# Three chained layers on one Trainium2 core: how v's scales are spread, and where w_in is decoded

## The chip, the cores and the metric

The program runs on one core of one Trainium2 chip. The metric is the device time of one execution in microseconds, as the median of three runs. The engines are named PE (matrix products), DVE (VectorE), ACT (ScalarE), POOL (GpSimd) and SP (the engine that issues nearly all DMA here, in program order).

## The reference

Three layers follow one another; the output of one is the input of the next. Four batches, 448 positions, 768 columns.

```python
# 1: attention, 12 heads of 64, mixing heads before and after the softmax
scores = scale * (q @ k.transpose(0, 1, 3, 2))
scores = np.einsum('bhij,hg->bgij', scores, w_pre)
attn = softmax(scores)
attn = np.einsum('bhij,hg->bgij', attn, w_post)
x = attn @ v
# 2: moe1
h = gelu_tanh(x @ w_in)
u, v = h[..., :512], h[..., 512:]
v_n = (v - mean(v)) / sqrt(var(v) + 1e-06) * g_ln
v_s = np.einsum('ts,bsd->btd', w_sg, v_n) + b_sg
x = x + (u * v_s) @ w_out
# 3: moe2
theta = x @ w_theta
y = np.einsum('ts,bsd->btd', w_tok_r, x * cos(theta)) + np.einsum('ts,bsd->btd', w_tok_i, x * sin(theta))
u = x + y
out = u + np.maximum(u @ w_ch, 0.0)
```

Five of the weights (w_in, w_out, w_theta, w_tok and w_ch) come as 64-bit floats and are turned on the chip into pairs of 32-bit tiles, a high and a low part, since a product takes three matmuls with them (high by high, high by low, low by high).

## The kernel before

**Attention** (function `attention`) goes through 180 blocks of up to 10 query rows by 12 heads. A block passes a chain of helpers, and the step loop (L437) issues in step s the helpers of several blocks at once, each with its own lookahead: `relayout(s+7)` (L217, a DMA that puts the scores of a block with heads on partitions), `premix(s+4)` (PE, L223, mixes heads) with `rowmax` (DVE nmx, L229), `expo(s+3)` (ACT e, L236), `recip2` and `p_hi(s+2)` (POOL ph, L255), `p_lo(s+1)` (DVE pl, L262), `postmix(s)` (PE, L277 to L280) and `at_hi`, `at_lo(s-1)` (ACT ah L302, DVE al L308). `attn_v` (L329) multiplies by v once a row of blocks is complete; `turn_x` and `store_x` transpose the result and store it to DRAM (xT). The lists `early`, `work` and `late` put other work into steps, and `tail` holds what stands in the steps relative to the last block, NB.

**v** is scaled for each batch and column by a power of two, so that a 16-bit high and low part hold it. `v_max` (L148) takes maxima of a transposed copy vT, with the columns on partitions; `v_scale` makes the scale sv, 128 partitions by 6. Scaling needs it along the free axis of all partitions. So `v_scale_out` (L162) writes sv to DRAM as 768 single elements, and `v_scale_in` (L166) reads them back to all 128 partitions as vbc. Then `v_mul` (POOL, L178), `v_hi` (ACT, L181) and `v_lo` (POOL, L185) make the two parts; in these steps lie what the prediction calls the stretches with v.

**Decode jobs** (class `Dense`, L573 to L631) each turn 128 by 256 numbers: a load (draw, L588), two ACT operations (L599, L600), two on DVE (L602, L604), one on DVE (L610), an ACT copy of the high part with a product on DVE or POOL (L615, L618), two on POOL (L624, L625), and, for jobs without a place of their own in SBUF, a store to DRAM (L631). Fourteen jobs stand beside attention, one each 11.6 steps: the 12 of the second half of w_in, and 2 of the first. They store to win_d in DRAM. The others are issued by `tick`, where each tick advances a pipeline whose steps lie apart by the numbers in LAGS; 15 ticks stand on the last steps of attention (5 before NB and on), and the tables TV, TU, TG and TO say how many follow each unit of moe1.

**moe1** (function `moe1`) is a list of units, which PE takes in order: `v_chunk` and `u_half` (w_in's second and first half), `gate` (w_sg), `out` (w_out), by batch. At the handover SP loads the second half of w_in back (`load_win`, L660), and x from xT (`load_x`, L742 and L744). **moe2** follows with theta, tok and ch; nearly all of it is matmuls.

Of the kernel before, what the change touches and what calls it, by code (L numbers as in the profile page):

```python
# [6 lines left out]
F32 = mybir.dt.float32  # L7
F32R = mybir.dt.float32r
# [9 lines left out]
NP = H // 2  # L18
DM = H * D
# [18 lines left out]
def attention(tc, nc, io, xT, B, extra, tail):  # L38
# [17 lines left out]
    with ExitStack() as es:  # L56
# [45 lines left out]
        ident = cp.tile([TI, TI], F32, name="ident")  # L102

        def consts():
            kpost = sm_p.tile([TI, H, IB], F32, tag="kpost", name="kpost", bufs=1)
            nc.sync.dma_start(out=kpost, in_=io["kpost"].rearrange("p (g i) -> p g i", g=H))
            nc.sync.dma_start(out=ident, in_=io["ident"][:TI, :TI])
# [33 lines left out]
        vs_dram = es.enter_context(tc.tile_pool(name="a_vsd", bufs=1, space=bass.MemoryType.DRAM))  # L141
        vs_d = vs_dram.tile([B, DM], F32, name="vs_d")
# [220 lines left out]
        def put(d, s, fn, *a):  # L363
            d.setdefault(s, []).append((fn, a))
# [119 lines left out]
TV = ((0, 1, 3, 1), (2, 2, 2, 2), (2, 1, 2, 2), (0, 1, 2, 0))  # L484
TU = ((2, 1, 0, 1), (2, 0, 2, 1), (2, 0, 2, 1), (3, 0, 2, 1))
TG = ((1, 0, 1, 0), (2, 1, 0, 1), (0, 1, 0, 1), (0, 1, 0, 0))
TO = ((2, 1, 1, 0, 1, 1), (0, 1, 0, 0, 2, 0), (0, 1, 1, 0, 0, 1), (0, 1, 1, 3, 2, 2))
KE = 1
# [5 lines left out]
LAGS = ((5, 7), (4, 5), (3, 4), (2, 3), (1, 2), (0, 0))  # L494
# [169 lines left out]
def moe1(d, left, right):  # L664
# [6 lines left out]
    def start():  # L671
# [6 lines left out]
        d.raw_bufs, d.mid_bufs, d.out_bufs = 3, 4, 4  # L678
# [8 lines left out]
        for k in range(KE, KD):  # L687
            def tiles(k=k):
                win[k, 0] = pair("win", HF, f"win{k}_0")
                return win[k, 0]  # L690
            d.jobs += d.decode_tiles(io["w_in"], slice(128 * k, 128 * k + 128), 0, HF, tiles)
        d.jobs += [None]
# [9 lines left out]
    def rest():  # L702
        tail_ps.close()
        for name, bufs in (("w", 1), ("u", 1), ("vn", 1), ("t", 2), ("dec", 1)):
            d.open(name, bufs, left)
        d.open_psum(8, right)
        w = d.pools["w"]
        gln = w.tile([128, KF], F32, name="gln")
        with nc.allow_non_contiguous_dma(reason="512 values"):
            nc.sync.dma_start(out=gln, in_=io["g_ln"].rearrange("(k p) -> p k", p=128))  # L710
# [9 lines left out]
    def load_win(k, half):  # L720
        win[k, half] = d.load_pair(d.pools["win"], d.win_d, slice(128 * k, 128 * k + 128),
                                   slice(HF * half, HF * half + HF), f"win{k}_{half}")
# [222 lines left out]
    return tail, win_es, g0[B - 1] - 1, end  # L945


def moe2(d, left, win_es, last_u, m1_left):
# [227 lines left out]
def build(tc, nc, io, out):  # L1176
    with tc.manual_schedule(), ExitStack() as top:
# [5 lines left out]
        right, left1, left2 = ExitStack(), ExitStack(), ExitStack()  # L1183
        tail, win_es, last_u, end = moe1(d, left1, right)
# [3 lines left out]
        jobs = d.decode_all(io["w_in"], HF, DFF, d.win_d)  # L1188
        jobs += d.decode_all(io["w_in"], 0, HF, d.win_d, 128 * KE)
# [4 lines left out]
        right.close()  # L1194
        left2.close()


def layout(i):
# [9 lines left out]
    for x in range(IB):  # L1208
# [14 lines left out]
        "g_ln": f(i["moe_g_ln"]),  # L1223
# [26 lines left out]
```

## Time and profile before

| | |
|---|---|
| median of 3 runs | 1046.14 us (1044.67 to 1046.32) |
| the profiled execution | 1047.47 us, its span 1045.6 us |
| mean granted clock of PE | 0.978 |
| PE busy | 982.3 us (94%) |
| DVE, POOL, ACT busy | 775.5, 622.4, 586.6 us |
| chain that ended last, by engine | PE 57%, DVE 20%, DMA 9%, POOL 5% |

PE is busy almost all of the time. An average over the whole span hides where it isn't, so the views below go by stretch: 0 to 60 us is the start, 60 to 470 the body of attention, 470 to 580 the handover and the first units of moe1, 580 to 740 the rest of it. From 800 on it is moe2.

### The profile page before, as it was taken

How to read it: one execution, taken by the hardware profiler on the slowest of the kernel's cores; microseconds unless marked ns; L12 is line 12 of the kernel's file. 1: busy time of each engine (PE TensorE's matmuls, PEld its weight loads, DVE VectorE, ACT ScalarE, POOL GpSimd, SP SyncE). 2: the span in 40 equal slices, each digit the busy share in tenths (PEclk: the TensorE clock that was granted, in tenths of full speed). 3: DMA queues.
4: the chain of work that ended last, by engine and by line, in shares of the span. 5: the costliest groups of instructions: out<-in, count | busy, mean ns of one | idle time of the engine just before them, and what ended most of it. 6: DMA issues, size and time to landing. Idle time of an engine off the chain costs nothing.

```text
span 1045.6 us, 21830 instructions
## 1 busy us (share of the span) xinstructions
PE 982.3 (94%) x7848; PEld 742.7 (71%) x7848; DVE 775.5 (74%) x1458; ACT 586.6 (56%) x1374; POOL 622.4 (60%) x818
## 2 busy tenths in 40 slices
PE   7789999999999999997978999799999999999998
PEld 2445655565656555566756979587888999999997
DVE  2799878987888878985989998898896724925611
ACT  4577778786777778775754645454364412613310
POOL 0596558754686548854656877775666643753622
PEclk9899999999999999998989999999999999999999
DMA  5757565556556564347353676758956131130021
GB/s 191 154 167 221 142 139 183 180 168 129 161 193 203 131 158 152 131 108 265 113 155 89 213 225 199 229 188 274 335 184 226 41 106 31 32 106 16 31 76 53
DMA packets 135504, 159.47 MB, mean 153 GB/s; under 512 B 30309, under 2 KB 120933, under 8 KB 135397
## 3 DMA queue, kind: packets, MB, share of 16 engines
q1 hardware_dynamic: 135397, 158.08, 50.3%
q8 instruction: 63, 1.03, 0.4%
q14 instruction: 44, 0.36, 0.1%
HBM read 86.66 MB, written 32.85 MB: 114 GB/s over the span
## 4 chain that ended last, share of the span: by engine, by line
PE 57%; DVE 20%; DMA 9%; POOL 5%; issue 4%; ACT 3%; SPq 1%; DVEq 0%; ACTq 0%; POOLq 0%
PE ps L564 27%; PE psB L223 10%; PE psA L203 5%; PE psD L329 5%; DVE da L604 3%; PE psC L280 3%; PE psC L277 3%; DMA blk<-s 2%; PE psC L278 2%; DVE pl L262 2%; DVE da L602 2%; DVE dp L610 2%; DMA xres<-xT 2%; DVE dp L618 2%; DMA xraw<-xT 1%
## 5 line engine op out<-in xcount | busy, mean ns | idle before, releaser
L255 POOL TENSOR_SCALAR ph<-e,rc 120x448 f16<-120x448 f32 x180 | 163.9, 911 | 147.3 <-DVE rc L250 99.8
L223 PE MATMUL psB<-blk,kpre 120*120 120x448 f32 x360 | 177.3, 575 | 13.0 <-DMA blk<-s 8.2
L229 DVE TENSOR_REDUCE nmx<-psB 120x1 f32<-120x448 f32 x180 | 111.3, 618 | 49.9 <-PE psB L223 40.8
L262 DVE SCALAR_TENSOR_TENSOR pl<-e,rc,ph 120x448 f16<-120x448 f32 x180 | 147.4, 819 | 0.0
L236 ACT ACTIVATE e<-psB,nmx 120x448 f32<-120x448 f32 x180 | 114.3, 635 | 43.1 <-DVE nmx L229 43.0
L308 DVE SCALAR_TENSOR_TENSOR al<-psC,ah 128x480 f16<-128x480 f32 x180 | 116.1, 645 | 8.2 <-ACT ah L302 7.9
L277 PE MATMUL psC<-wh,ph 120*128 120x120 f16 x720 | 97.7, 218 | 10.9 <-DVE al L308 7.1
L302 ACT ACTIVATE ah<-psC 128x480 f16<-128x480 f32 x180 | 103.0, 572 | 7.6 <-PE psC L280 4.9
L209 ACT ACTIVATE s<-psA 120x896 f32<-120x896 f32 (+1 forms) x90 | 82.5, 917 | 42.5 <-PE psA L203 41.1
L564 PE MATMUL ps<-wtok,z 128*128 128x448 f32 x504 | 104.8, 368 | 0.4 <-POOL z L560 0.4
L564 PEld LDWEIGHTS ps<-wtok,z 128*128 128x128 f32 x504 | 94.4, 188 | 10.1 <-POOL z L560 0.8
L277 PEld LDWEIGHTS <-ph 120*128 120x128 f16 x720 | 68.8, 99 | 44.3 <-issue 18.6
L278 PE MATMUL psC<-wl,ph 120*128 120x120 f16 x720 | 97.1, 218 | 2.4 <-issue 2.4
L329 PEld LDWEIGHTS <-ah 128*128 128x128 f16 x1536 | 76.6, 99 | 31.2 <-issue 31.2
L203 PE MATMUL psA<-k,q 64*120 64x448 f32 (+1 forms) x384 | 96.2, 580 | 1.0 <-ACT s L209 1.0
L564 PE MATMUL ps<-wth,x2s 128*128 128x384 f32 x504 | 92.5, 338 | 2.0 <-POOL x2s L560 2.0
L564 PE MATMUL ps<-u,wch 128*128 128x448 f32 x432 | 89.9, 368 | 0.0
L564 PEld LDWEIGHTS ps<-wth,x2s 128*128 128x128 f32 x504 | 87.2, 188 | 2.8 <-POOL x2s L560 2.6
L560 POOL TENSOR_TENSOR z<-zz,z 128x384 fp32r<-128x384 f32 x56 | 61.9, 1125 | 45.8 <-ACT z L557 45.8
L564 PEld LDWEIGHTS ps<-u,wch 128*128 128x128 f32 x432 | 81.0, 188 | 8.1
L278 PEld LDWEIGHTS <-ph 120*128 120x128 f16 x720 | 71.2, 99 | 14.4 <-issue 14.2
L329 PE MATMUL psD<-vl,ah 128*128 128x64 f16 x768 | 78.0, 194 | 1.1 <-POOL vl L185 1.1
(124 smaller groups left out, 2171.9 us busy)
## 6 DMA issues: line engine op xcount, KB each, us to landing
blk<-s SPq DMA_DIRECT2D x176, 210.0 KB
draw<-in_w_in SPq DMA_DIRECT2D x24, 256.0 KB
vraw<-in_vN SPq DMA_DIRECT2D x24, 256.0 KB
k<-in_kvT SPq DMA_DIRECT2D x24, 224.0 KB
vT<-in_kvT SPq DMA_DIRECT2D x12, 448.0 KB
xraw<-xT SPq DMA_DIRECT2D x24, 224.0 KB
xres<-xT SPq DMA_DIRECT2D x24, 224.0 KB
x2T<-xres SPq DMA_DIRECT2D x24, 224.0 KB
```

The costliest lines, as they stand in the source:

```text
L203: nc.tensor.matmul(ps[e][:n, :S], q[p, o:o + n], k[p], start=True, stop=True)
L223: nc.tensor.matmul(ps[:r, :S], kpre[:r, :r], sblk.pop(s)[:r], start=True, stop=True)
L229: nc.vector.tensor_reduce(out=m[:r], in_=mix[s][:r, :S], axis=AX.X, op=ALU.max, negate=True)
L236: nc.scalar.activation(out=e[:r], in_=mix.pop(s)[:r, :S], func=AF.Exp, bias=nmx.pop(s)[:r], accum_out=sm[:r])
L255: nc.gpsimd.tensor_scalar(out=p[:r], in0=ex[s][0][:r], scalar1=rec[s][:r], scalar2=0.0, op0=ALU.mult, op1=ALU.add)
L262: nc.vector.scalar_tensor_tensor(out=p[:r], in0=ex.pop(s)[0][:r], scalar=rec.pop(s)[:r], in1=ph[s][:r], op0=ALU.mult, op1=ALU.subtract)
L277: nc.tensor.matmul(ps[:, jc, :, :n], cols(a, jc), wh[:r, :, :n], start=(jc == 0), stop=False)
L278: nc.tensor.matmul(ps[:, jc, :, :n], cols(a, jc), wl[:r, :, :n], start=False, stop=False)
L302: nc.scalar.activation(out=at_view(s, at[b, t][0]), in_=src, func=AF.Copy, scale=2.0 ** -17)
L308: nc.vector.scalar_tensor_tensor(out=al, in0=src, scalar=2.0 ** -17, in1=ah, op0=ALU.mult, op1=ALU.subtract)
L329: nc.tensor.matmul(ps[:, o:o + 64], a[:, i0:i0 + 128], v[:, jc, 64 * e:64 * e + 64], start=(o == 0 and m == 0), stop=(o == 320 and m == le ...
L564: self.nc.tensor.matmul(ps, l, r, start=(i == 0), stop=(i == len(terms) - 1))
```

## The change

v's scales no longer go through DRAM. `v_diag` writes them onto the diagonals of six 128x128 tiles (ACT), and `v_spread` multiplies these by a tile of ones in two matmuls of 384 columns, each followed by an ACT copy from PSUM (buffer psT, one of it) to vbc. vT is loaded two steps later at the start, and its maxima stand in steps -2 to 0.

All 24 jobs of w_in stand beside attention. The 12 of the second half come first and write their tiles straight into SBUF, in a new pool w1 that is open from the beginning; for such jobs the product of L618 is always on DVE. The 12 of the first half still store to win_d, and six loads bring them back, two steps apart, at steps NB-4 to NB+6. Three ticks are left on attention's last steps, w_out's jobs come first there, and the tables are spread anew. The pool w1 later holds the first half of w_theta and the last 128 columns of w_ch. g_ln comes transposed, so that its load is contiguous. Middle buffers of the jobs are 3 for 4, output buffers 5 for 4.

```diff
-        def v_scale_out(b):
-            with nc.allow_non_contiguous_dma(reason="768 scales"):
-                nc.sync.dma_start(out=vs_d[b].rearrange("(c p) -> p c", p=128), in_=raws.pop(("sv", b)))
-
-        def v_scale_in(b):
-            bc = vsc_p.tile([128, DM], F32, tag="vbc", name="vbc", bufs=1)
-            nc.sync.dma_start(out=bc, in_=vs_d[b].partition_broadcast(128))
-            vsb[b] = bc
+        def v_diag(b):
+            sv = raws.pop(("sv", b))
+            raws["dg", b] = vsc_p.tile([128, NP, 128], F32R, tag="dg", name="dg", bufs=1)
+            for c in range(NP):
+                nc.scalar.activation(out=raws["dg", b][:, c], in_=ident, func=AF.Copy, scale=sv[:, c:c + 1])
+
+        def v_spread(b):
+
+            dg = raws.pop(("dg", b))
+            vsb[b] = vsc_p.tile([128, DM], F32, tag="vbc", name="vbc", bufs=1)
+            for half in range(2):
+                ps = psD.tile([128, 512], F32, tag="psT", name="psV", bufs=1)
+                nc.tensor.matmul(ps[:, :384], ones, dg[:, 3 * half:3 * half + 3], start=True, stop=True)
+                nc.scalar.activation(out=vsb[b][:, 384 * half:384 * half + 384], in_=ps[:, :384], func=AF.Copy)
...
             put(late, s, v_scale, b)
-            put(early, s + 2, v_scale_out, b)
-            put(early, s + 5, v_scale_in, b)
+            put(late, s + 1, v_diag, b)
+            put(work, s + 2, v_spread, b)
...
-            put(early, -LD + c // 2, load_vT, 0, c)
-            put(late, -LD + 1 + c // 2, v_max, 0, c)
-        put_v(0, -LD + 4, VM, 2)
+            put(early, -LD + 2 + c // 2, load_vT, 0, c)
+            put(late, -2 + c // 2, v_max, 0, c)
+        put_v(0, 1, VM, 2)
...
-LAGS = ((5, 7), (4, 5), (3, 4), (2, 3), (1, 2), (0, 0))
+LAGS = ((5, 6), (4, 4), (2, 3), (3, 3), (1, 2), (0, 0))
...
-        d.raw_bufs, d.mid_bufs, d.out_bufs = 3, 4, 4
+        d.raw_bufs, d.mid_bufs, d.out_bufs = 3, 3, 5
...
+    def decode_win():
+
+        jobs = []
+        for k in range(KD):
+            def tiles(k=k):
+                t = d.pools["w1"].tile([128, 2, HF], F32R, tag=f"w1_{k}", name=f"win{k}_1")
+                win[k, 1] = t[:, 0], t[:, 1]
+                return win[k, 1]
+            jobs += d.decode_tiles(io["w_in"], slice(128 * k, 128 * k + 128), HF, DFF, tiles)
+        return jobs + d.decode_all(io["w_in"], 0, HF, d.win_d)
...
-        at(-6 + k // 3, load_win, k, 1)
+        at(-4 + 2 * k, load_win, k)
         at(-6 + k // 2, load_x, 0, k)
         at(-5 + k // 2, split_x, 0, k)
-    for k in range(KE):
-        at(-4, load_win, k, 0)
-    for i in range(17 - 2 * KE):
-        at(-6 + KE + i, d.tick)
+    for i in range(3):
+        at(5 + 2 * i, d.tick)
...
-        jobs = d.decode_all(io["w_in"], HF, DFF, d.win_d)
-        jobs += d.decode_all(io["w_in"], 0, HF, d.win_d, 128 * KE)
```

Three places show how the order moves. First SP at the start, from the last load of vT on; vs_d and vbc are the two ends of the round trip, draw the first decode job's load. Before:

```order
L133 DMA vT<-in_kvT 128x2x448
L217 DMA blk<-s 120x1x448 x4
L162 DMA vs_d<-sv 128x6x1
L217 DMA blk<-s 120x1x448 x2
L588 DMA draw<-in_w_in 128x512
L217 DMA blk<-s 120x1x448
L166 DMA vbc<-vs_d 128x768
L217 DMA blk<-s 120x1x448
L173 DMA vraw<-in_vN 128x4x128
```

and after:

```order
L135 DMA vT<-in_kvT 128x2x448
L223 DMA blk<-s 120x1x448 x4
L593 DMA draw<-in_w_in 128x512
L223 DMA blk<-s 120x1x448 x2
L179 DMA vraw<-in_vN 128x4x128
L223 DMA blk<-s 120x1x448
L140 DMA q<-in_qT 128x720
```

The two issues of the round trip are gone from between the blk issues. Next SP at the handover, from the last blk on; win_1 is the second half of w_in, win_0 the first, xraw a piece of x. Before:

```order
L217 DMA blk<-s 96x1x448
L685 DMA ident<-in_ident 128x128
L660 DMA win_1_9143<-win_d 128x2x512
L742 DMA xraw<-xT 128x448
L744 DMA xraw<-xT 128x64
L660 DMA win_1_9148<-win_d 128x2x512
```

and after:

```order
L752 DMA xraw<-xT 128x64
L665 DMA win_0_9464<-win_d 128x2x512
L750 DMA xraw<-xT 128x448
L752 DMA xraw<-xT 128x64
L750 DMA xraw<-xT 128x448
L752 DMA xraw<-xT 128x64
L364 DMA xT<-x 128x3x120
L665 DMA win_0_9550<-win_d 128x2x512
L665 DMA win_0_9620<-win_d 128x2x512
```

The loads of x now go first, and the loads of w_in that are left are those of the first half, further back. Last DVE just before the first wsg (the spatial gate's weight, made there); da and dp are operations of decode jobs, v the normalised half of moe1. Before:

```order
L618 TENSOR_TENSOR dp<-dp,dl 128x256
L610 TENSOR_SCALAR dp<-da 128x256
L782 RECIPROCAL sd<-sd 128x4
L618 TENSOR_TENSOR dp<-dp,dl 128x256
L602 TENSOR_SCALAR da<-dp 128x256
L604 SCALAR_TENSOR_TENSOR da<-dp,da 128x256
L787 TENSOR_SCALAR v<-v,mv,sd 128x512 x2
L610 TENSOR_SCALAR dp<-da 128x256
L602 TENSOR_SCALAR da<-dp 128x256
L604 SCALAR_TENSOR_TENSOR da<-dp,da 128x256
L787 TENSOR_SCALAR v<-v,mv,sd 128x512 x2
L560 TENSOR_TENSOR wsg<-wsgraw,wsg 128x448 x2
```

and after:

```order
L781 BN_STATS bst<-v 128x6
L784 BN_AGGR mv<-bst 128x2
L790 RECIPROCAL sd<-sd 128x4
L795 TENSOR_SCALAR v<-v,mv,sd 128x512 x2
L607 TENSOR_SCALAR da<-dp 128x256
L609 SCALAR_TENSOR_TENSOR da<-dp,da 128x256
L795 TENSOR_SCALAR v<-v,mv,sd 128x512 x2
L565 TENSOR_TENSOR wsg<-wsgraw,wsg 128x448 x2
```

Between the last nmx and this wsg DVE has the first two operations of 12 jobs before and of 1 after; from there to the first xres it is 12 before and 14 after, and from xres to the end 48 and 47.

## Rows read from the trace of the kernel before

**Rows 1.** busy time by stretch: length, engines (instructions), TensorE clock, DMA share, GB/s

```profile
0.00:60.00 60.00, 46.54 (x244) 21.01 (x244) 33.30 (x75) 32.52 (x68) 20.86 (x37) 0.94 0.61 164
60.00:470.00 410.00, 393.65 (x4684) 239.77 (x4682) 346.40 (x717) 314.03 (x755) 265.15 (x430) 1.00 0.56 162
470.00:580.00 110.00, 91.45 (x689) 74.95 (x687) 92.60 (x173) 62.54 (x158) 64.11 (x75) 0.89 0.50 157
580.00:740.00 160.00, 151.20 (x673) 127.44 (x672) 139.32 (x228) 80.64 (x194) 120.42 (x137) 0.97 0.72 230
```

**Rows 2.** timeline of SP near the first scale round trip: start, length, issue

```profile
26.74 0.38 SPq L162 DMA_DIRECT2D vs_d<-sv  x1
...
36.90 0.35 SPq L166 DMA_DIRECT2D vbc<-vs_d  x1
```

**Rows 3.** PE timeline, batches 0 and 1: start, length, [idle before <- releaser]

```profile
38.57 1.82 PE L223 MATMUL psB<-blk,kpre 120*120 120x448 f32 x2 [5.38 <-DMA blk<-s]
...
143.48 0.98 PE L223 MATMUL psB<-blk,kpre 120*120 120x448 f32 x2 [0.95 <-DMA blk<-s]
```

**Rows 4.** busy time by stretch, at the scales of batches 0, 2, 3

```profile
38.00:44.00 6.00, 5.43 (x27) 3.43 (x28) 3.49 (x8) 1.88 (x6) 1.28 (x2) 0.50 1.01 257
254.00:258.00 4.00, 1.85 (x14) 0.80 (x12) 0.00 (x0) 0.56 (x2) 0.80 (x2) 1.00 0.59 107
370.00:374.00 4.00, 2.02 (x23) 1.24 (x21) 0.43 (x3) 1.22 (x5) 0.95 (x2) 1.00 0.51 95
```

**Rows 5.** timeline of DVE at the start, before the first block

```profile
19.80 1.09 DVE L148 TENSOR_REDUCE vmx<-vT 128x2 f32<-128x896 f32 x1 [7.20 <-DMA vT<-in_kvT]
...
22.94 0.61 DVE L229 TENSOR_REDUCE nmx<-psB 120x1 f32<-120x448 f32 x1
```

**Rows 6.** groups of instructions, 60 to 470 us: busy us, mean ns | idle

```profile
L333 ACT ACTIVATE xi<-psD 120x384 f32<-120x384 f32 (+1 forms) x28 | 13.7, 490 | 11.9 <-PE psD L329 11.9
L625 POOL TENSOR_TENSOR dh<-da,dp 128x256 fp32r<-128x256 f32 x13 | 12.5, 964 | 1.0
...
L624 POOL TENSOR_TENSOR da<-da,dh 128x256 f32<-128x256 f32 x13 | 9.4, 726 | 1.0
...
L604 DVE SCALAR_TENSOR_TENSOR da<-dp,da 128x256 uint32<-128x256 uint32 x13 | 7.5, 575 | 0.4
...
L602 DVE TENSOR_SCALAR da<-dp 128x256 uint32<-128x256 uint32 x13 | 5.6, 433 | 0.7 <-ACT dp L599 0.7
...
L618 DVE TENSOR_TENSOR dp<-dp,dl 128x256 f32<-128x256 f32 x5 | 4.2, 845 | 0.0
L610 DVE TENSOR_SCALAR dp<-da 128x256 uint32<-128x256 uint32 x13 | 3.7, 283 | 0.0
```

**Rows 7.** the page, costliest groups: one row

```profile
L564 PE MATMUL ps<-wth,x2s 128*128 128x384 f32 x504 | 92.5, 338 | 2.0 <-POOL x2s L560 2.0
```

**Rows 8.** chain of waits, 186 to 194 us: start, length, what

```profile
187.31 1.29 DVE da L602
...
188.63 0.74 DVE da L604
```

**Rows 9.** timeline of POOL, the same place

```profile
186.79 1.65 POOL L178 TENSOR_TENSOR vraw<-vraw,vbc 128x512 f32<-128x512 f32 x1
```

**Rows 10.** busy time by stretch, one with v work and one without

```profile
160.00:200.00 40.00, 37.36 (x383) 21.42 (x379) 35.17 (x67) 31.10 (x81) 32.80 (x46) 0.96 0.50 158
200.00:250.00 50.00, 50.00 (x632) 31.18 (x629) 43.00 (x94) 39.41 (x91) 26.93 (x50) 1.00 0.65 178
```

**Rows 11.** PE's waits, 470 to 492 us: total, times, longest

```profile
PE psC L277 <- DVE al L308: 7.1, 2, 5.1
```

**Rows 12.** busy time by stretch, handover and first gates

```profile
484.00:492.00 8.00, 6.07 (x54) 5.49 (x53) 2.50 (x5) 2.75 (x5) 3.76 (x5) 0.51 1.06 374
531.00:548.00 17.00, 10.82 (x31) 7.15 (x30) 16.83 (x23) 11.31 (x28) 13.49 (x14) 0.70 0.38 117
```

**Rows 13.** timeline of PE at the first output matmul of moe1

```profile
570.24 7.10 PE L564 MATMUL ps<-g,wout 128*128 128x448 f32 x26 [3.33 <-POOL wout L625]
```

More of the change, by code (lines that the diff above doesn't have):

```diff
@@ L101, in attention @@
         dwp = cp.tile([128, NP], F32, name="dwp")
-        ident = cp.tile([TI, TI], F32, name="ident")
+        ident = cp.tile([128, 128], F32, name="ident")
+        ones = cp.tile([128, 128], F32R, name="ones")
         def consts():
@@ L106, in consts @@
             nc.sync.dma_start(out=kpost, in_=io["kpost"].rearrange("p (g i) -> p g i", g=H))
-            nc.sync.dma_start(out=ident, in_=io["ident"][:TI, :TI])
+            nc.sync.dma_start(out=ident, in_=io["ident"])
+            nc.scalar.activation(out=ones, in_=ident, func=AF.Copy, scale=0.0, bias=1.0)
             wrep = sm_p.tile([128, H, H], F32, tag="wrep", name="wrep", bufs=1)
@@ L140, in attention @@
         vt, dsc, vsb = {}, {}, {}
-        vs_dram = es.enter_context(tc.tile_pool(name="a_vsd", bufs=1, space=bass.MemoryType.DRAM))
-        vs_d = vs_dram.tile([B, DM], F32, name="vs_d")
         def v_max(b, c):
@@ L483 @@
 E_G = ('PPPV', 'VVPP', 'VPVP', 'VVPV')
[L484 to L488, printed above, removed]
+TV = ((), (2, 2, 2), (1, 1, 1, 1), (1, 1, 1))
+TU = ((1, 1, 1, 1), (2, 1, 2, 1), (2, 1, 2, 1), (2, 1, 2, 1))
+TG = ((1, 1, 1, 1), (0, 1, 0, 1), (0, 1, 0, 1), (0, 0, 0, 0))
+TO = ((1, 1, 1, 1, 1, 1), (1, 1, 1, 1, 1, 1), (1, 1, 1, 0, 1, 1), (0, 0, 1, 1, 1, 1))
 MAGIC = 12582912.0
@@ L686, in start @@
         pair = lambda pool, n, tag: [d.pools[pool].tile([128, n], F32R, tag=f"{tag}_{i}", name=tag) for i in range(2)]
[L687 to L692, printed above, removed]
         for k in range(KF):
@@ L708, in rest @@
         gln = w.tile([128, KF], F32, name="gln")
-        with nc.allow_non_contiguous_dma(reason="512 values"):
-            nc.sync.dma_start(out=gln, in_=io["g_ln"].rearrange("(k p) -> p k", p=128))
+        nc.sync.dma_start(out=gln, in_=io["g_ln"])
         bsg = w.tile([128, S], F32, name="bsg")
@@ L718, in rest2, with load_win @@
             d.open(name, bufs, left)
-    def load_win(k, half):
-        win[k, half] = d.load_pair(d.pools["win"], d.win_d, slice(128 * k, 128 * k + 128),
-                                   slice(HF * half, HF * half + HF), f"win{k}_{half}")
+    def load_win(k):
+        win[k, 0] = d.load_pair(d.pools["win"], d.win_d, slice(128 * k, 128 * k + 128), slice(0, HF), f"win{k}_0")
+    def decode_win():
[7 more added lines that the diff above has]
+        return jobs + d.decode_all(io["w_in"], 0, HF, d.win_d)
     def load_wsg(c):
@@ L944, in moe1 @@
         at(8 + c // 2, norm, 0, c)
-    return tail, win_es, g0[B - 1] - 1, end
+    return tail, decode_win(), win_es, g0[B - 1] - 1, end
 def moe2(d, left, win_es, last_u, m1_left):
@@ L958, in load_wth @@
     def load_wth(k, half):
-        wth[k, half] = d.load_pair(d.pools["th"], d.wth_d, slice(128 * k, 128 * k + 128),
-                                   slice(384 * half, 384 * half + 384), f"wth{k}_{half}")
+        rows = slice(128 * k, 128 * k + 128)
+        if half:
+            wth[k, 1] = d.load_pair(d.pools["th"], d.wth_d, rows, slice(384, DM), f"wth{k}_1")
+            return
+        t = d.pools["w1"].tile([128, 1024], F32R, tag=f"w1_{k}", name=f"wth{k}_0")
+        th, ch = (t[:, c].rearrange("p (i n) -> p i n", i=2) for c in (slice(0, 768), slice(768, 1024)))
+        nc.sync.dma_start(out=th.bitcast(F32), in_=d.wth_d[:, rows, :384].rearrange("i p c -> p i c"))
+        wth[k, 0] = th[:, 0], th[:, 1]
+        wch[k, 1] = ch
     def rest():
@@ L971, in load_wtok, with load_wch @@
                                                         slice(0, S), f"wtok{c}")
-    def load_wch(k, half):
-        wch[k, half] = d.load_pair(d.pools["wch"], d.wch_d, slice(128 * k, 128 * k + 128),
-                                   slice(384 * half, 384 * half + 384), f"wch{k}_{half}")
+    def load_wch(k, part):
+        rows = slice(128 * k, 128 * k + 128)
+        if part == 0:
+            wch[k, 0] = d.load_pair(d.pools["wch"], d.wch_d, rows, slice(0, 640), f"wch{k}")
+        else:
+            ch = wch[k, 1]
+            nc.sync.dma_start(out=ch.bitcast(F32), in_=d.wch_d[:, rows, 640:].rearrange("i p c -> p i c"))
+            wch[k, 1] = ch[:, 0], ch[:, 1]
     def sine_table():
@@ L1101, in ch @@
         uh, ul = ut[b]
-        half, o = divmod(128 * m, 384)
+        half, o = divmod(128 * m, 640)
         fs = slice(o, o + 128)
@@ L1182, in build @@
         d.scratch(dram)
-        right, left1, left2 = ExitStack(), ExitStack(), ExitStack()
-        tail, win_es, last_u, end = moe1(d, left1, right)
+        right0, right, left1, left2 = (ExitStack() for _ in range(4))
+        d.open("w1", 1, right0, "right")
+        tail, jobs, win_es, last_u, end = moe1(d, left1, right)
         th_es = moe2(d, left2, win_es, last_u, left1)
@@ L1194, in build @@
         right.close()
+        right0.close()
         left2.close()
@@ L1222, in layout @@
         "w_in": w64(i["moe_w_in"]),
-        "g_ln": f(i["moe_g_ln"]),
+        "g_ln": f(i["moe_g_ln"].reshape(KF, 128).T),
         "w_sgT": f(i["moe_w_sg"].T),
```

## The prediction, on record before the changed kernel ran

> **What bounds the kernel now.** I read the busy time by stretch first [rows 1]. PE is the engine to look at: it is busy for 393.65 of the 410 us between 60 and 470, and at full clock there. So work taken off another engine is worth something only where PE stands still or runs at half clock. The reader should form two numbers for each stretch: length less PE busy time (idle), and PE busy time times one less the clock (lost to the clock). 0 to 60 us has 13.5 us idle and 2.8 of clock; 60 to 470 has 16.4 idle; 470 to 580 has 18.6 idle and 10.1 of clock; 580 to 740 has 8.8 and 4.5. (The clock is rounded to 0.01, so these are good to half a microsecond.) What any edit can give is in these. The rest of the program, moe2 above all, isn't touched in its order.
>
> Then I went to the places. At the start SP issues the write of the scales at 26.74 us, and the read back, which waits for it, at 36.90 [rows 2]. SP takes its issues in order, so the blocks' relayouts (blk) behind the waiting read can't be issued, and PE stands 5.38 us for blk at 38.57; the premix pair that follows takes 1.82 us, against 0.98 for the same pair at full clock [rows 3], and the clock stays at half for the next 6 us [rows 4]: 5.43 busy us at 0.50, so 2.7 us lost. This repeats smaller for each batch: 0.95 us before a premix in batch 1 [rows 3], and in batches 2 and 3 stretches of 4 us with 1.85 and 2.02 us of PE work [rows 4], that is 2.15 and 1.98 idle.
>
> At the handover from attention to moe1 PE waits 7.1 us for al, in two waits [rows 11], and 484 to 492 us runs at 0.51 with the DMA engines full (share 1.06) [rows 12]. At the first gates it has 10.82 busy us in 17 at a clock of 0.70 [rows 12], while DVE is busy for 16.83 of the 17; and the first output matmul waits 3.33 us for the last w_out tile [rows 13].
>
> **The change, part by part** (a minus is time gained; the sum is made on the profiled execution, 1047.47 us).
>
> *The first scale round trip* goes: its 5.4 idle and 2.7 of clock are at SP's blocked queue, and no DMA stands in the scales' way any more. Two smaller things move with it. The three maxima of vT (1.09 us each on DVE) no longer stand before the first nmx: now the first is waited for (7.20 us) at 19.80 and the first nmx follows at 22.94 [rows 5]. That could start the pipeline up to about 3 us earlier. But the same three maxima and the scale arithmetic (about 1 us) now stand between steps, where DVE paces the first steps: 3 x 1.09 + 1 = 4.3 us back. So -8.1 - 3 + 4.3 = **-7**, bounds -3 (half of the stall returns as a wait of the tightened first steps) and -10.
>
> *The other three round trips* go: 0.95 + 2.15 + 1.98 = **-5**, bounds -4 and -5.
>
> *The spread* that replaces them: six ACT copies of 128x128 (not in this trace; the 128x384 eviction is 490 ns [rows 6], and a 128x128 copy is a third of that in columns, so 6 x 0.2 to 0.5) and, on PE, two matmuls of 384 columns, each with its eviction to SBUF by ACT. The nearest matmul takes 338 ns [rows 7]. There is one PSUM buffer (psT) for both, so the second matmul waits for the first's eviction: PE loses 2 x 0.34 and about 0.5 to 1 us of waiting per batch, four times: 4 x 1.5 = **+6**, bounds +3 (waits hidden) and +9 (ACT's six copies also delay an exponential).
>
> *Ten more decode jobs beside attention.* Before, 14 jobs over 162 steps, one each 11.6 steps; after, 24, one each 6.75. A job costs DVE 0.433 + 0.575 + 0.283 + 0.845 = 2.14 us (the last multiplication now always on DVE for the twelve jobs that write tiles in place) and POOL 0.726 + 0.964 = 1.69 [rows 6]. What does it cost PE? Two kinds of stretch differ. Where v isn't scaled PE is the bound: 50.00 of 50 us, with DVE at 43.00 and POOL at 26.93 [rows 10]; here a job fits into 7 us of slack per 50 and costs nearly nothing, 0.3 to 0.5 us. Where v is scaled, DVE is at 35.17 and POOL at 32.80 of 40, PE at 37.36 [rows 10]; and a job there shows on the chain of waits: 1.29 us for an operation whose mean is 0.433, then 0.74 [rows 8], right beside a POOL product of 1.65 us [rows 9]. A job in such a stretch is worth 2 to 2.5 us. These stretches are about 160 of 410 us; by the order, about 12 of 24 jobs touch one after and 8 of 14 before. So 4 x 2.3 + 6 x 0.4 = **+12**. The bounds: +5 (all ten at 0.5) and +26 (all ten at 2.6).
>
> *The handover.* Before, six loads of 512 KB of the second half of w_in stand between the loads of x on SP, and 15 decode ticks lie on the attention's last steps. After, the second half is in SBUF already, x is loaded first, the six loads of the first half follow two steps apart, and three ticks are left. The 7.1 us of waits for al and half of the 6.07 busy us at 0.51 (3.0) are charged to that [rows 11, 12]. It gives **-10**; bounds -12 and -6 (six loads still come, only later, and x is still stored and read back).
>
> *First gates and outputs.* By DVE's order twelve jobs stood between the last nmx and the first wsg, and one is left. But fourteen instead of twelve stand from wsg to the first xres: DVE, full there, has two jobs more (2 x 2.3 us), and w_out's tiles, on which PE waits at 570.24, now start later against PE. What is gained is that wsg isn't queued behind decodes and that gln's load is contiguous. Of 6.2 idle, 3.2 of clock [rows 12] and 3.33 [rows 13] I take **-5**, bounds 0 (the waits move to w_out) and -13.
>
> *Later*: the jobs from xres to the end are 47 for 48, with one middle buffer less, one output buffer more and shorter lags. The stretch 580 to 740 has 8.8 us idle to win from [rows 1]: **-2**, bounds -8 and +3 (three middle buffers make ACT wait).
>
> The sum: -7 - 5 + 6 + 12 - 10 - 5 - 2 = -11, so 1036.5 us for the profiled execution. That one is 1.3 us above the median of the runs, 1046.14; against the median I forecast **1035 us**.
>
> **Rivals.**
>
> *R1, the jobs hide and the gates close.* If shorter SP queues leave DVE's slack where the jobs fall, they cost +5 instead of +12, and the first gates give -13 instead of -5: 1035 - 7 - 8 = 1020. For it: the stretches without v take a job for nothing. Against: DVE has twelve jobs to do for w_out before PE may pass, and it is full where PE waits.
>
> *R2, DVE and POOL serialise (slower than before).* Two DVE operations beside POOL's 1.65 us product took 1.29 and 0.74 us for 0.433 and 0.575 [rows 6, 8, 9]. If the ten jobs all fall under such locking, each costs what DVE and POOL need one after the other, 2.14 + 1.69 = 3.83 us, so +38 instead of +12, and the time is 1035 + 26 = 1061. It decides from where a moved job costs PE 2.3 us on average: then the ten cost 23 and the forecast's gain of 11 is used up. For it: POOL is busier beside v too, and the twelve jobs in place put the product on DVE always. Against: 200 to 250 us lost nothing at all with jobs in it [rows 10]. The Trainium skill ("SBUF — State Buffer", section "SBUF: two separate sides") speaks for this rival: VectorE and GpSimd share a port pair as an exclusive lock, and an operation of VectorE with two SBUF inputs and one of GpSimd shut each other out for their whole length. By that rule nearly all of a job's operations on the two engines would add up; the trace agrees at 187 us, where da took three times its mean beside vraw, and not at 200 to 250.
>
> *R3, the stalls move.* The start's first steps stay bound by DVE (-3 for -7) and the handover by x's round trip (-6 for -10): 1035 + 4 + 4 = 1043. For it: x is still stored and reloaded through DRAM there, and PE waits for al, a DVE product behind ACT, not for a load.
>
> **How the numbers follow.** Forecast 0.53, R1 0.18, R3 0.15, R2 0.14. The forecast's own terms scatter by the larger of their bounds (start and handover +4 each, jobs +14 or -7, gates +5 or -8); they won't all end on one side, and two thirds of it lie within 1026 to 1044. So the range, which takes in the forecast, R3 and the nearer end of R1 and leaves out most of R2, is 1018 to 1047. A difference of 0.2%, about 2.1 us, is what a measurement of this kernel can tell from none. Faster than 1044.0: forecast 0.49, R1 0.18, R3 0.09, that is 0.76; within 1044.0 to 1048.2: 0.03 and 0.05, so 0.08; slower: 0.14 for R2 and 0.02 of the rest, 0.16.
>
> **What would show it.** At the start: no wait of PE for blk over 1 us, clock at 1.00 from 30 to 60 us, and psV matmuls with a wait of about 0.5 us at the second. Between 60 and 470: idle grows from 16.4 us to about 29, with decode pieces on the chain in the stretches with v; if it stays under 20, R1; if it is over 40, R2, with DVE's da and dp at twice their means. At the handover: PE's wait for al under 2 us and the clock above 0.9; if x's arrival is what PE waits for, R3. At the first gates: wsg right when its load lands, and a wait of PE for wout still there. The prediction is wrong if attention from 60 on grows by more than 20 us, or if the start keeps its stall with another name.

## The result, and the profile after

The changed kernel took 1059.65 us (median of 4 runs, 1059.29 to 1059.89), against 1046.23 us for the kernel before in the same comparison: 1.0134 times as long, with a 95% interval of 1.0115 to 1.0152. It is **13.4 us slower**, where 1035 us was forecast.

First the busy time by stretch after the change, the view of [rows 1]: length, busy time of PE, PEld, DVE, ACT and POOL with the number of instructions, the granted clock of PE, the DMA share and GB/s.

```profile
0.00:60.00 60.00, 48.92 (x278) 21.47 (x278) 38.68 (x87) 39.63 (x88) 25.78 (x43) 1.00 0.53 169
60.00:470.00 410.00, 387.75 (x4565) 235.26 (x4564) 346.35 (x723) 318.93 (x777) 271.99 (x432) 0.98 0.52 159
470.00:580.00 110.00, 97.52 (x770) 77.43 (x767) 80.96 (x141) 56.45 (x138) 50.80 (x61) 0.91 0.44 125
580.00:740.00 160.00, 148.62 (x659) 123.79 (x657) 141.03 (x233) 82.43 (x198) 116.46 (x137) 0.97 0.67 209
```

Beside [rows 1] the start and the handover are better: 2.4 us less idle in the first 60 us with the half clock gone, 6.1 us less in 470 to 580. The body of attention is worse: 22.3 us idle for 16.4, and its clock is no longer 1.00.

Stretches by time drift apart once one kernel is late. So the same point of the program has to be set against itself. DVE's first operation of each block (nmx) marks the steps of attention; these are the marks of block 15 and of the last block, 179, in the timeline of DVE after the change (start, length, operation):

```profile
55.43 0.61 DVE L235 TENSOR_REDUCE nmx<-psB 120x1 f32<-120x448 f32 x1
...
485.96 0.62 DVE L235 TENSOR_REDUCE nmx<-psB 96x1 f32<-96x448 f32 x1 [0.27 <-PE psB L229]
```

and before:

```profile
60.51 0.61 DVE L229 TENSOR_REDUCE nmx<-psB 120x1 f32<-120x448 f32 x1
...
475.61 0.62 DVE L229 TENSOR_REDUCE nmx<-psB 96x1 f32<-96x448 f32 x1 [0.26 <-PE psB L223]
```

With PE's timeline for the units of moe1, the account of the two profiled executions reads so (each line is the difference gained or lost between two marks):

| from, to | after less before, us | the prediction's terms for it |
|---|---|---|
| start to block 15 | -5.1 | -7 + 1.5 (a quarter of the spread) |
| block 15 to block 179 | +15.4 | -5 + 4.5 + 12 |
| block 179 to the end of batch 0's u | -7.9 | -10 |
| to the end of the first three output units | +0.7 | -5 |
| to the end of the span | +9.0 | -2 |

The sum is +12.2, the difference of the spans (1057.8 and 1045.6); the lines are rounded. They are single executions, and such a stretch scatters: block 15 to block 179 took 415.1 us here, and 410.9 to 413.2 us in three kernels of the experiments that have the same attention. Attention lost about what three terms together said, and nearly all of the error seems to lie behind the handover. The runs below show that this is half of it: within attention two terms are wrong that cancel.

**Attention.** PE's waits over the whole span, after (total, times, longest):

```profile
PE ps L569 <- DVE x L565: 12.0, 6, 3.8
PE psC L286 <- DVE pl L268: 11.9, 19, 1.5
PE psV L172 <- ACT vbc L173: 8.1, 4, 2.5
PE ps L569 <- POOL x L565: 3.5, 3, 1.7
```

psV are the spread's matmuls. The second of each pair waits for ACT's copy of the first, 2 us each time and not 0.5 to 1. Batch 2's pair in PE's timeline, then ACT's timeline at that place:

```profile
246.69 0.45 PE L172 MATMUL psV<-dg,ones 128*128 128x384 f32 x1
249.65 0.69 PE L172 MATMUL psV<-dg,ones 128*128 128x384 f32 x1 [2.51 <-ACT vbc L173]
```

```profile
245.65 1.86 ACT L164 ACTIVATE dg<-ident,sv 128x128 fp32r<-128x128 f32 x6 [0.89 <-DVE sv L94]
247.42 0.41 ACT L604 ACTIVATE dp<-draw 128x256 f32<-128x256 f32 x1
247.74 0.42 ACT L605 ACTIVATE dl<-draw 128x256 f32<-128x256 uint32 x1
248.06 0.61 ACT L242 ACTIVATE e<-psB,nmx 120x448 f32<-120x448 f32 x1
248.58 0.19 ACT L242 ACTIVATION_READ_ACCUMULATOR e<-psB,nmx 120x1 f32 x1
248.67 0.56 ACT L308 ACTIVATE ah<-psC 128x480 f16<-128x480 f32 x1
249.12 0.47 ACT L173 ACTIVATE vbc<-psV 128x384 f32<-128x384 f32 x1
```

The copy itself takes 0.47 us. Between the matmul's end and the copy ACT does a decode job's two operations, an exponential and ah, because they stand before the copy in its order. In PE's timeline nothing of what stands behind the second matmul runs during its 2.51 us. In batches 2 and 3 what follows costs as much again. The busy time by stretch for the 6 us after batch 2's pair, and for 8 us from batch 3's second matmul on:

```profile
250.00:256.00 6.00, 6.00 (x43) 3.36 (x42) 0.77 (x2) 3.08 (x6) 1.23 (x2) 0.50 0.00 0
...
372.00:380.00 8.00, 6.94 (x47) 3.94 (x47) 2.15 (x6) 4.09 (x10) 1.50 (x4) 0.57 0.23 75
```

PE is busy all of the first stretch at a granted clock of 0.50, the lower of its two levels: 3 us lost there, and 3 in the second (6.94 busy us at 0.57).

**moe1.** x of batch 1 is late. PE's timeline at its products:

```profile
554.76 1.65 PE L569 MATMUL ps<-win,x 128*128 128x512 f32 x3 [3.83 <-DVE x L565]
```

The wait at 570.24 for w_out [rows 13] is gone, and this came in its place, while DVE, as before at the first gates [rows 12], has no time left (busy time by stretch):

```profile
549.00:567.00 18.00, 10.40 (x27) 7.48 (x28) 17.59 (x25) 6.12 (x15) 11.26 (x12) 0.62 0.14 41
```

And a wait turns up that the kernel before hardly had. ACT's waits from 520 to 740 us, after:

```profile
ACT dh L620 <- DVE da L609: 44.8, 31, 3.0
ACT wout L620 <- DVE da L609: 24.3, 9, 4.2
```

and before:

```profile
ACT wout L615 <- DVE da L604: 6.8, 5, 3.3
...
ACT dh L615 <- DVE da L604: 4.0, 4, 1.3
```

69 us in 40 waits for 11 us in 9. This is ACT's copy of a job's high part, waiting for DVE's da of the same job. The rows overstate the growth: before the change the same copy stood another 23 us for other things, most of it output buffers whose store hadn't landed. With all causes ACT's idle time just before this copy, between 520 and 740 us, is 33.8 us before and 69.2 after.

### The profile page after: what moved, and what is told of

It is laid out like the page before. It is cut to its first block, busy times and chain, and to the rows that moved or that the text cites. A ratio compares the mean times of both kernels' runs of the same rounds, so it can differ in the third digit from the quotient of the medians.

```text
span 1057.8 us, 21843 instructions
## 1 busy us (share of the span) xinstructions
PE 991.0 (94%) x7856; PEld 745.3 (70%) x7856; DVE 777.6 (74%) x1459; ACT 597.4 (56%) x1407; POOL 621.7 (59%) x817
## 4 chain that ended last, share of the span: by engine, by line
PE 54%; DVE 20%; DMA 8%; POOL 6%; ACT 6%; issue 4%; SPq 1%; DVEq 0%; POOLq 0%; ACTq 0%
PE ps L569 26%; PE psB L229 8%; PE psA L209 6%; PE psD L335 5%; DVE da L609 3%; DVE da L607 3%; PE psC L283 2%; PE psC L286 2%; DVE pl L268 2%; PE psC L284 2%; DMA xres<-xT 2%; DVE dp L615 2%; POOL ph L261 2%; DVE dp L623 2%; DMA blk<-s 2%
## 5 line engine op out<-in xcount | busy, mean ns | idle before, releaser
L261 POOL TENSOR_SCALAR ph<-e,rc 120x448 f16<-120x448 f32 x180 | 167.9, 933 | 137.5 <-DVE rc L256 73.3
L268 DVE SCALAR_TENSOR_TENSOR pl<-e,rc,ph 120x448 f16<-120x448 f32 x180 | 149.6, 831 | 0.0
L283 PEld LDWEIGHTS <-ph 120*128 120x128 f16 x720 | 68.4, 98 | 44.7 <-POOL rc L250 17.7
L209 PE MATMUL psA<-k,q 64*120 64x448 f32 (+1 forms) x384 | 98.7, 594 | 0.7 <-ACT s L215 0.6
L569 PE MATMUL ps<-win,x 128*128 128x512 f32 x252 | 70.4, 436 | 16.4 <-DVE x L565 12.0
L286 PE MATMUL psC<-wh,pl 120*128 120x120 f16 x720 | 68.5, 219 | 12.3 <-DVE pl L268 11.9
L335 PE MATMUL psD<-vh,ah 128*128 128x64 f16 x768 | 79.1, 195 | 0.0
L335 PE MATMUL psD<-vh,al 128*128 128x64 f16 x768 | 78.6, 194 | 0.0
```

What stands on the lines that cost most here:

```text
L209: nc.tensor.matmul(ps[e][:n, :S], q[p, o:o + n], k[p], start=True, stop=True)
L261: nc.gpsimd.tensor_scalar(out=p[:r], in0=ex[s][0][:r], scalar1=rec[s][:r], scalar2=0.0, op0=ALU.mult, op1=ALU.add)
L268: nc.vector.scalar_tensor_tensor(out=p[:r], in0=ex.pop(s)[0][:r], scalar=rec.pop(s)[:r], in1=ph[s][:r], op0=ALU.mult, op1=ALU.subtract)
L283: nc.tensor.matmul(ps[:, jc, :, :n], cols(a, jc), wh[:r, :, :n], start=(jc == 0), stop=False)
L335: nc.tensor.matmul(ps[:, o:o + 64], a[:, i0:i0 + 128], v[:, jc, 64 * e:64 * e + 64], start=(o == 0 and m == 0), stop=(o == 320 and m == le ...
L569: self.nc.tensor.matmul(ps, l, r, start=(i == 0), stop=(i == len(terms) - 1))
```

## The experiments

The theory after reading the two traces: the spread costs attention its time, not the ten jobs; and the shorter lags (LAGS) cost moe1 its own. The rivals: R2 of the prediction (the jobs serialise DVE and POOL), and for moe1 the denser tables of ticks. Ratios are to the kernel before, run on the same chip each time. A difference between two kernels is that of two such ratios and carries both intervals, some 3 us together; "by the marks" means the stretches of the table above, in single profiled executions.

**The round trip back for batches 1 to 3** (changed kernel):

```diff
-            put(late, s + 1, v_diag, b)
-            put(work, s + 2, v_spread, b)
+            if b:
+                put(early, s + 2, v_scale_out, b)
+                put(early, s + 5, v_scale_in, b)
+            else:
+                put(late, s + 1, v_diag, b)
+                put(work, s + 2, v_spread, b)
```

> The changed kernel, but the scales of batches 1 to 3 go through DRAM again (written and read back by SP); batch 0 keeps the spread. Theory A (the spread, not the ten jobs, is what slows attention): of the 15.5 us that attention loses between block 15 and block 179, 13.0 lie at the three spreads (2.3, 6.4 and 4.3 us by the blocks' times), so the time falls to 1046.6 us (1044 to 1050), and psV waits are left once. Rival B (the ten more decode jobs slow attention, and PE would wait at these places for something else): it stays above 1055 us.

Measured: 1.0037 (1.0015 to 1.0058) for 1.0134, some 10 us less, with one psV wait left:

```profile
PE psV L184 <- ACT vbc L185: 1.5, 1, 1.5
```

By the marks, block 15 to block 179 takes 417.3 us for 430.5. So the slow DRAM round trip was cheaper than what replaced it, and the spreads explain most of attention's loss. It was also cheaper than the -5 us of the prediction: with three round trips in it, PE's waits from 60 to 465 us hold this,

```profile
PE psB L241 <- issue: 0.4, 1, 0.4
PE psB L241 <- DMA blk<-s: 0.2, 1, 0.2
```

where `issue` is idle time for which the profile shows no cause. Most of the idle time of [rows 4] that the prediction charged to the round trips of batches 2 and 3 has no other name in the kernel before either (PE's waits from 369 to 375 us there):

```profile
PE psC L278 <- issue: 1.6, 1, 1.6
PE psC L277 <- issue: 0.3, 1, 0.3
```

**The spread's two matmuls in steps of their own** (changed kernel):

```diff
-            put(work, s + 2, v_spread, b)
+            put(work, s + 3, v_spread, b, 0)
+            put(work, s + 5, v_spread, b, 1)
```

> The changed kernel, but the spread's two matmuls stand three and five steps after the scales, in steps of their own, instead of in a row two steps after. Theory A (PE stands because the first matmul waits for ACT's six copies and the second for ACT's eviction, and then runs at half clock): the waits at psV (10.6 us in 7) go under 2 us, and the half clock after them too (about 6 us), so 1043 to 1048 us. Rival: the added instructions cost that much wherever they stand: above 1055 us.

Measured: 1.0060 (1.0037 to 1.0083), 7.7 us less than the changed kernel. No wait at psV is left; what turned up is a transposition that finds psT taken, in PE's waits:

```profile
PE psT L349 <- ACT vbc L174: 2.3, 3, 0.8
```

Most of the spread's price was its place, not its amount of work: two matmuls in a row with one buffer, and between them all that ACT has queued. The edit moves the first matmul back as well as the second away from it, so it doesn't tell the wait for dg (2.5 us of the 10.6) from the wait for the eviction. Nor does it show that the spread, well placed, gains on the round trip: 1.0060 is no better than 1.0037 above.

**Ticks of batch 0's gates on its u units** (changed kernel):

```diff
-TU = ((1, 1, 1, 1), ...
-TG = ((1, 1, 1, 1), ...
+TU = ((2, 2, 2, 2), ...
+TG = ((0, 0, 0, 0), ...
```

> The changed kernel, but the four ticks of batch 0's gates stand on its four u units (two each for one). Theory T (batch 1's x waits for DVE since four ticks instead of two stand among these gates): PE's wait for x in batch 1 (7.8 us and as much at half clock) falls to under 3 us, and the time to 1050 to 1055 us. Rival L (the shorter lags make ACT wait for DVE inside each tick, and x's cast stands behind that): 1058 us or more. It may also give part back at wsg, which these ticks now precede.

Measured: 1.0147 (1.0111 to 1.0182). Nothing gained in time. PE's waits from 500 to 600 us, in the changed kernel and in this one:

```profile
PE ps L569 <- DVE x L565: 7.8, 3, 3.8
PE ps L569 <- DVE vn L565: 1.7, 1, 1.7
```

```profile
PE ps L569 <- ACT x L562: 4.7, 1, 4.7
PE ps L569 <- ACT vn L562: 3.5, 1, 3.5
PE ps L569 <- DVE x L565: 2.8, 4, 1.5
```

The wait that theory T named fell under 3 us, as it said. But ACT's casts of x and vn came late instead, as rival L's sign had it for x, and the sum is no smaller. So the ticks' place decided which wait PE had there, and not how long it stood.

**The changed lags and buffers in the kernel before:**

```diff
-LAGS = ((5, 7), (4, 5), (3, 4), (2, 3), (1, 2), (0, 0))
+LAGS = ((5, 6), (4, 4), (2, 3), (3, 3), (1, 2), (0, 0))
...
-        d.raw_bufs, d.mid_bufs, d.out_bufs = 3, 4, 4
+        d.raw_bufs, d.mid_bufs, d.out_bufs = 3, 3, 5
...
-        d.jobs += [None]
+        d.jobs += [None, None]
```

> The kernel before, with the changed kernel's lags and buffers (three middle, five output) and one empty tick more ahead of w_out's jobs, so that their tiles come in the same ticks as before. Rival L: it is 6 us or more slower than before (1052 us and up), with x of batches 1 and 2 late. Theory T: within 2 us of before (1044 to 1048 us).

Measured: 1.0120 (1.0083 to 1.0158). These lines, put into a kernel that has nothing else of the change, cost it about 12.5 us, as much as the whole change did. That the totals agree is chance, for the places differ. By the marks, from the last block to the end of the first three output units this kernel loses 6.5 us against the kernel before (108.1 for 101.6), and 5.8 us behind them; the changed kernel gains 7.2 us in the first of these and loses 9.0 in the second. Here 15 ticks stand on attention's last steps, there three.

**Lags and buffers of before in the changed kernel:**

```diff
-LAGS = ((5, 6), (4, 4), (2, 3), (3, 3), (1, 2), (0, 0))
+LAGS = ((5, 7), (4, 5), (3, 4), (2, 3), (1, 2), (0, 0))
...
-        d.raw_bufs, d.mid_bufs, d.out_bufs = 3, 3, 5
+        d.raw_bufs, d.mid_bufs, d.out_bufs = 3, 4, 4
...
-    for i in range(3):
-        at(5 + 2 * i, d.tick)
+    for i in range(4):
+        at(3 + 2 * i, d.tick)
```

> The changed kernel with the lags of before, four middle buffers (three for dl, the one tile that is done earlier) and four output buffers, and four ticks instead of three on attention's last steps, so that w_out's tiles come in the same ticks. Theory L (the shorter lags make ACT's copy of the high part wait for DVE's da of the tick just before, and x's cast and the gates stand behind it): ACT's waits for da (69 us in 40 between 520 and 740) go under 15 us, PE's waits for x (15.5 us in 9) under 5 us, and the time falls by about as much as these lags cost the kernel before, 12 us: 1045 to 1050 us. Rival D (the denser tables cost it, whatever the lags): 1055 us or more.

Measured: 1.0050 (1.0037 to 1.0064), 8.8 us less than the changed kernel. ACT's waits from 520 to 740 us:

```profile
ACT dh L620 <- DVE da L609: 7.2, 9, 1.5
...
ACT wout L620 <- DVE da L609: 4.1, 4, 2.1
```

11 us for 69, and 26.3 for 69.2 with all causes. By the marks, what lies behind the first three output units takes 467.4 us, for 477.4 in the changed kernel and 468.4 before: the lags and buffers are all of the +9.0 there. PE's waits for x of batches 2 and 3 shrink with them, and a smaller one for g turns up (580 to 700 us, first this kernel, then the changed one):

```profile
PE ps L569 <- DVE x L565: 3.0, 1, 3.0
PE ps L569 <- POOL g L565: 2.5, 1, 2.5
PE ps L569 <- POOL x L565: 1.0, 2, 0.7
```

```profile
PE ps L569 <- DVE x L565: 4.2, 3, 2.2
PE ps L569 <- POOL x L565: 3.5, 3, 1.7
```

But x of batch 1 is as late as ever: in the three waits of that batch PE loses 1.86, 2.27 and 3.63 us. The expectation that this goes too was wrong; that wait isn't the lags'.

**Both: the old lags and the spread apart** (the edits of the two kernels above together).

> The same, and the spread's matmuls in steps of their own. If the two causes add up: 8 us less than with the lags alone, about 8 us faster than before (1036 to 1041 us), which would be the whole of what the forecast of 1035 expected. If one hides behind the other (moe1 is bound by DVE's work, and an earlier start of it only waits longer): within 3 us of the lags alone.

Measured: 1036.32 us, 0.9931 (0.9911 to 0.9951). The two causes at least add up (0.74% and 0.84% alone, 2.0% together; the excess is within the intervals), and this kernel **beats both**, about 7 us below the kernel before. By the marks it gains 6.7 us up to block 15 and 8.8 from the last block to the end of the first three output units, and 0.7 behind them. From block 15 to block 179 it still loses 3.7. So the start and the handover carry the gain, and two details of the change hid it. The old lags with the round trip back in batches 1 to 3 weren't tried; that kernel may be as fast or faster.

**Without the ten jobs' work** (changed kernel, 14 jobs beside attention; each load of the first half also reads rows 0 to 127 only):

```diff
-        return jobs + d.decode_all(io["w_in"], 0, HF, d.win_d)
+        return jobs + d.decode_all(io["w_in"], 0, HF, d.win_d)[:2]
```

> The changed kernel without the ten jobs that moved (14 beside attention): the ten jobs' decoding of w_in's first half is left out, and all six loads of it read the two blocks that are decoded. Prices the ten jobs. By the prediction's term (1.2 us each) the time falls by 12 us to 1048 us; by the blocks' times outside the spreads (2.5 to 3 us for all ten) to 1056 to 1058 us; by rival R2's 3.8 us each it would be 1022 us.

Measured: 1.0093 (1.0066 to 1.0120), 4.3 us below the changed kernel, with intervals that overlap a little: 1 to 8 us, and not 12. By the marks attention is 8.6 us shorter in this execution (422.0 for 430.5), and 4.0 of it are lost again behind the last block. So the ten jobs' price isn't known to better than a few us, but R2's 38 is ruled out. What goes is what they do to pl, in PE's waits between 60 and 470 us, with 24 jobs and with 14:

```profile
PE psC L286 <- DVE pl L268: 9.3, 15, 1.5
```

```profile
PE psC L286 <- DVE pl L268: 3.8, 8, 0.8
```

The psV waits stay (6.6 us for 6.3 in the row there): they don't need the jobs.

**The changed lags alone in the kernel before** (its own four and four buffers):

```diff
-LAGS = ((5, 7), (4, 5), (3, 4), (2, 3), (1, 2), (0, 0))
+LAGS = ((5, 6), (4, 4), (2, 3), (3, 3), (1, 2), (0, 0))
...
-        d.jobs += [None]
+        d.jobs += [None, None]
```

> The kernel before with the changed lags and the empty tick, but with its own buffers (four middle, four output). Theory L: the lags alone carry it, so it is as slow as with the changed buffers too, 1.0 to 1.4% above before. Rival M (three middle buffers, not the lags, make ACT wait): within 0.3% of before.

Measured: 1.0168 (1.0144 to 1.0191). The lags carry it and not the buffers. It is more than the 1.0 to 1.4% expected; with the changed buffers it was 1.0120, with an interval that overlaps this one, so what the buffers do beside the lags stays open.

**The high part's step, and the store, one tick nearer** (kernel before):

```diff
-LAGS = ((5, 7), (4, 5), (3, 4), (2, 3), (1, 2), (0, 0))
+LAGS = ((5, 6), (4, 5), (2, 3), (3, 3), (1, 2), (0, 0))
...
-        d.jobs += [None]
+        d.jobs += [None, None]
```

> The kernel before with its own buffers and the empty tick, and of the lags only the high part's step (ACT's copy of da, with the product beside it) and the store one tick nearer: lags 3 and 6 for 4 and 7. The low part's step on POOL keeps its lag of 5. Theory L, made narrower (it is ACT's copy, which now follows DVE's da by one tick and not by two, that holds ACT): 1.0 to 1.7% slower than before, as with all the lags changed, with ACT's waits for da at 40 us or more. Rival P (the low part's step, POOL waiting for ACT, carries it): within 0.4% of before.

Measured: 1.0154 (1.0133 to 1.0176). The low part's lag, which is as before here, isn't needed for the loss. The store isn't either, as far as its distance to the low part goes: that is one tick here and two in the kernel with all the lags changed, which is as slow. So the high part's step, one tick nearer, is what is left; a kernel with that alone wasn't run. By the marks 7.8 us are lost from the last block to the end of the first three output units and 9.1 behind them. ACT's waits from 520 to 740 us there, less than the 40 us expected but three times those of before:

```profile
ACT dh L615 <- DVE da L604: 18.8, 12, 3.2
...
ACT wout L615 <- DVE da L604: 12.8, 8, 2.1
```

With all causes ACT stands 57.4 us before this copy, for 33.8 in the kernel before.

Three more were made on the kernel with both mended, where PE still waits 8.0 us for x of batch 1. There DVE is busy for 4.53 of the 20 us before the u units, since w_out's tiles have no place in SBUF until then and only four ticks can run, and for 17.76 of 18 us when x is wanted (busy time by stretch):

```profile
486.00:506.00 20.00, 20.00 (x237) 16.75 (x237) 4.53 (x10) 5.99 (x17) 0.00 (x0) 1.00 0.28 90
...
534.00:552.00 18.00, 9.99 (x29) 6.83 (x30) 17.76 (x28) 7.04 (x17) 11.03 (x12) 0.81 0.20 59
```

The three edits, in order: E_X for batch 1; the same as in the third experiment; and TU, TG and TV for batches 0 and 1.

```diff
-E_X = ('VVVPPP', 'VPVVVP', ...
+E_X = ('VVVPPP', 'PPVPVP', ...
```

> The changed kernel with the old lags and the spread apart, and two of the four x remainders of batch 1 that stood on DVE put on POOL (PPVPVP for VPVVVP). In that kernel PE still waits 8 us for x of batch 1 between 534 and 552 us, where DVE is busy for 17.76 of 18 us and POOL for 11.03. If DVE's work there is what x waits for, these waits fall by half and the time by 3 to 6 us against the same kernel without it (1.0% below before). If x waits for POOL or ACT just as long, it stays within 2 us.

```diff
-TU = ((1, 1, 1, 1), ...
-TG = ((1, 1, 1, 1), ...
+TU = ((2, 2, 2, 2), ...
+TG = ((0, 0, 0, 0), ...
```

> The same kernel (old lags, spread apart), with the four ticks of batch 0's gates on its u units. With the short lags this moved nothing. If it is only DVE's total of decode work up to batch 1's x that counts, it moves nothing here either (within 2 us); if the ticks' place counts, x of batch 1 comes earlier and 4 to 8 us are gained.

```diff
-TV = ((), (2, 2, 2), ...
-TU = ((1, 1, 1, 1), ...
-TG = ((1, 1, 1, 1), ...
+TV = ((), (2, 3, 2), ...
+TU = ((2, 1, 1, 1), ...
+TG = ((1, 0, 1, 0), ...
```

> The same kernel (old lags, spread apart), with one tick more on batch 0's u units, two fewer on its gates and one more on v of batch 1: one job less of DVE's work ahead of batch 1's x. If the total of decode work ahead of x counts, about one tick (2.3 us and some half clock) is gained, 2 to 4 us; it is lost again if out(0, 0) then waits for w_out.

Measured: 0.9934, 0.9941 and 0.9940, all with intervals that hold 0.9931. None of them moved the time. PE's waits between 500 and 600 us show what came instead. With two remainders on POOL the wait for x falls to 5.9 us, and the clock of 470 to 580 us is lower (0.89 for 0.94); but the profiled execution took 1040.63 us, 5 us above that kernel's median, so this reading is weak. With the ticks on u, and with one tick moved behind, the waits change their names:

```profile
PE ps L571 <- DVE x L567: 4.9, 4, 3.2
PE ps L571 <- DVE wsg L567: 3.3, 1, 3.3
```

```profile
PE ps L571 <- DVE wsg L567: 3.4, 1, 3.4
PE ps L571 <- DVE x L567: 2.7, 3, 1.4
```

8.2 and 6.1 us in these two rows, for 8.0 in the one row before (x alone). So the order of DVE's work hardly matters there. That its amount sets the limit isn't shown: with one job less ahead of x, the last kernel is 3.0 us earlier from the last block to the end of the first three output units (89.7 for 92.7), but loses 2.4 us behind them and gains nothing in the median. Whether more decoding beside attention would help wasn't tried, and what makes batch 1's x late stays open.

## Why the prediction was wrong, by its own steps

**The start** was right: -5.1 for -7, with the wait for blk at 38.57 [rows 3] and the half clock [rows 4] gone (38 to 44 us runs at 1.00 after); a wait for blk of 2.1 us at 28.59 is left.

**The spread** is the first step that failed. The price of its parts was near: a psV matmul took 0.44 us, six copies 1.86 us. The wait was taken as "about 0.5 to 1 us" a batch and bounded by +9 in all; it was 2.0 us at the second matmul, 2.6 with the first's wait for dg (10.6 us in four batches), and the clock halved behind two of them. ACT's order was there to be read: between the six copies and the first eviction stand an exponential and ah, and in batch 2 a decode job's pair. The eviction was priced by its own length, and not by what is queued ahead of it on its engine, nor by what PE holds back meanwhile. In batches 1 to 3 the spread cost about 10 us more than the round trip it replaced, where the sum had it at -0.5 (three quarters of +6, less 5). Part of that is the -5 itself, **the other three round trips**: with them back, PE waited 0.2 us for blk and 0.4 without a cause. In the kernel before only batch 1's 0.95 us [rows 3] had the name of a DMA; the 4.1 us of batches 2 and 3, which lay near the read back, were charged to SP too.

**The ten jobs** were probably mis-sized the other way: +12 for a measured 4 (1 to 8). R2, which would have made them +38, gives almost the measured time (1061 for 1060), and it is not why. Without the ten jobs' work the kernel is still 0.9% slower than before. The Trainium skill ("SBUF — State Buffer", section "SBUF: two separate sides") describes the exclusive lock of VectorE and GpSimd on which R2 rested. The trace agrees that single operations stretch, as L602 in [rows 8, 9], and pl's waits above grow with the jobs. But L602 reads one tile and not the two inputs of R2's sentence. And the second operation that R2 read beside the product, L604 at 188.63, ran after it: vraw had ended at 188.44. The jobs' price here was some 0.4 us each, a tenth of the 3.83.

**The handover** was right: -7.9 for -10. **The first gates and outputs** gave +0.7 for -5. The gates took 14.3 us for 20.6, with one wait of 1.7 us left, and PE then waited 7.8 us for batch 1's x instead, which the working named only as two more jobs of DVE's time. The wait for wout that it expected to stay was gone.

**Later** is the second step that failed: -2, with bounds of -8 and +3, for a measured +9.0, and -1.0 with the old lags and buffers back. The lags were named in that term and not costed; its upper bound had ACT wait for the three middle buffers, but in the kernel before the lags alone cost 1.7%, without these buffers. Shortened, the high part's copy follows da by one tick where it had two. DVE is full there and runs behind; ACT arrives early, stands, and with it all that stands behind it on ACT: x's cast, the gates' copy, the next job's first two operations. This chain is read from ACT's order and its waits; which of these operations costs PE how much wasn't taken apart. The row to look for was ACT's wait for da, 11 us in 9 between 520 and 740 us before the change, which a shorter lag was likely to lengthen.

The wrong terms of attention cancelled (+11.5 for a measured +15.4), so a forecast of the stretch alone would have looked nearly right, by luck. It is the runs that told them apart.

## What to carry to other kernels

A matmul that waits for an eviction waits for all that stands ahead of it on the evicting engine, so put dependent pairs of it into different steps. (Two buffers might do the same; that wasn't tried.) The lag between two steps of a software pipeline on different engines is slack that the slower engine uses up; price a shorter lag by that engine's backlog, and not by the length of the step. And look at a change with good and bad parts in it by its parts: here the parts that stayed were worth 7 us, and two details of some 8 and 9 us hid them.

## What the runs showed of the hardware

How long PE stood didn't say by itself whether its clock fell. After batch 2's wait of 2.51 us the granted clock was 0.50 for 6 us, and after batch 3's waits of 1.25 and 1.88 us it was 0.57 over 8 us; after batch 0's, of 0.77 and 1.87 us, and batch 1's, of 0.45 and 1.87 us, it stayed at 1.00 (30 to 60 and 128 to 136 us). And the slow-looking round trip of 768 single elements through DRAM, 10 us from issue to issue [rows 2], made PE wait hardly at all in its three later places (0.2 us for blk in the kernel with the round trip back), some 10 us less than two short matmuls in the wrong place.
